# A gated state-space convolution and squared-ReLU MLP with all gradients: where one activation buffer lies, where the last row block of the MLP's backward pass is emitted, and a stored copy of (1-g)G

## The chip, the cores and the metric

The kernel runs on one core of a Trainium2 chip. Its metric is the device time of one execution in microseconds (us), as the median of several runs. Engines are called TensorE (PE in the profile), VectorE (DVE), ScalarE (ACT), GpSimd (POOL) and SyncE (SP).

## The reference

Inputs are u (2048 x 448, called x in the MLP), the parameters of a diagonal state-space model with 256 states for each of the 448 channels, the weights w1 (448 x 1792), b1, w2 (1792 x 448), b2, a gate vector and the gradient G of the output. Computed are the output and the gradients of all inputs:

```
g  = sigmoid(sum(x * gate_w))                     # one number per row
K  = Re(sum_n C * dB * exp(l * dt * A))           # a filter of 2048 taps per channel
a  = irfft(rfft(u, 4096) * rfft(K, 4096))[:2048] + u * Dskip
h  = relu(x @ w1 + b1);  b = (h * h) @ w2 + b2
out = g * a + (1 - g) * b
return out, vjp(out)(G)                           # out and its gradients
```

With L = 2048, D = 448, F = 1792, P = 128 there are LT = 16 row tiles, FT = 14 tiles of F, DT = 4 tiles of D; a row block is 512 rows, so there are four of them.

## The kernel before, in words

The program is written in a framework that gives each engine its own instruction order, worked out from the order in which the Python code emits the work and from data dependencies. Those become semaphore waits between engines. An `issue_after` forces one instruction to be placed after another. Memory comes as named tiles (X16, Y16, D16, U16, K28, R32, F17, P14, M8, S25), each of which exists once: taking the same tag again waits for the last users of the overlapping part of it. The profile names tiles by the first letter, so F is F17. PSUM is split into banks N0 to N3, X, S and the double bank F. SB is the tile S25, and RA is R32.

Stages, in order of time:

1. *FFT of u and of g·G (0 to about 190 us).* `fwd1` (L222) makes a first stage of matrix products, stores it to DRAM (gd), `load_s1` (L241) reads it back turned, `fwd2` (L243) makes the second stage; spectra are multiplied (`cmul`, L263 to L268) and transformed back (`inv1`, L270, to hd in DRAM). Between them transposes of u and of DB = (1-g)·G are stored (`transposed`, UT_d and DBT_d). DB itself is made at L518 by ScalarE in tile D16. `powers` (L588) makes records of powers of the state matrix in two sets of buffers, one of which lies in the tile F17 (`Fp`), and stores them as rec_d. The first row block of the MLP's hidden layer is made here: `hidden(0, jp, ...)` (L543, called at L647) does a matrix product into PSUM, then on ScalarE a Relu (L559) into a ring buffer r of 1024 columns and its square (L561) into SB; the ring buffer is stored to DRAM as rT_d by GpSimd (L565). The ring has two buffers: the end of the w1 tile in U16, and `Fp[:,7680:8704]`.
2. *K's gradient.* Constants Ew and Ew2 are loaded (L651 to L654, Ew2 in SB), hd is read back (`load_hs`, L291: tiles D and P), L671 sums it on TensorE into DK, which goes through DRAM (dk_d, L681 to L688).
3. *Recurrence (213 to 660).* A loop over 14 chunks of the states (L906). For each chunk VectorE builds tables X and Y from the records by products of powers (`build_x` and `build_y`, L715 to L776, with ScalarE's L756, L757, L765, L767 preparing factors in tile F); TensorE makes taps of K from them (`kgen`, L789; stored to k_d at L803) and the state gradients: `turn_yt` (L827, L828), `tables_t` (L815, L816), `back_z` (L857, L861), and `back_p` (L864), where VectorE forms products (L877, four per chunk) in buffers `Pr` and TensorE sums them (L886, 32 per chunk, sixteen for each half). Into this loop the scheduler mixes the MLP: forward (`hidden` and `project`, L936 to L948, results to br_d), w1 and w2 transposed (L969, L979), and backward (L996 to L1021). A backward row block is 56 matrix products dh = DB·w2^T (L1005, L1008) in banks N0 to N2, ScalarE's doubling (L1010), VectorE's product with r (L1017), which is read from rT_d into a ring `rr` (L993), GpSimd's store to dhT_d (L1018), and then `project` (56 matrix products, L946, evacuation L947, store to br_d L948).
4. *K's FFT.* The taps k_d are read back with 18 loads of SP (L1092 to L1097, tile X), a skip term is added (L1100), `fwd1` (L232) makes the first stage with a ring of 6 stage buffers in Y16 and P14, the stores go to gd, `load_s1` (L1182) reads them into K. At its end SP also loads spectra (R<-sp), the gradient (Y<-grad_out) and br_d. From L1107 on `act_only` is set, with which all evacuations of PSUM are ScalarE's.
5. *Products, inverse transforms, outputs, and the weights' gradients.* `grad_w2` (L1060) and `grad_w1` (L1065) call `gradrows` (L1051), sixteen matrix products (L1057) per tile of F; DB2 is DB once more, made from four loads of G into D16 and sixteen ScalarE scalings (L1084). `param_grads` (L1145) ends the program.

Of the kernel before, what the change touches and what calls it, by code (L numbers as in the profile page):

```python
# [19 lines left out]
P = 128  # L20
# [285 lines left out]
def kernel(ctx, tc, A_u, A_A_re, A_A_im, A_B_re, A_B_im, A_C_re, A_C_im, A_log_dt, A_Dskip,  # L306
# [17 lines left out]
    UT_d = dscr("UT_d", DP * L)  # L324
    k_d = dscr("k_d", VROW * D)
# [17 lines left out]
    def flat(ap):  # L343
        return ap.rearrange("p t d -> p (t d)")
# [172 lines left out]
    for t in range(LT):  # L517
        S.activation(DB[:, t, :], G[:, t, :], ACT.Copy, scale=omg32[:, t:t + 1])  # L518
    ps = K.ps("S", [P, 512])
# [127 lines left out]
    for jp in range(6):  # L647
        hidden(0, jp, NT[4:6], [w1v[:, 7168:8192], Fp[:, 7680:8704]])
# [64 lines left out]
    Pr = [b[:, 2048 * i:2048 * i + 2048].rearrange("p (s t g n) -> p s t g n", t=2, s=2, g=2) for b, k in ((Pt, 3), (P2, 1)) for i in range(k)]  # L713
# [150 lines left out]
    def back_p(c, XT, zb, gs, after):  # L864
# [8 lines left out]
        for r in range(2):  # L873
            pr = Pr[pi_ % 4]
# [58 lines left out]
    ring = [w1v[:, 7168:8192], Fv[:, 2048:3072], Fv[:, 3072:4096]]  # L933
    ni = 0

    def project(lb, w, hblk, ws, brs):  # L936
        nonlocal ni
        for tt in range(4):
            t = 4 * lb + tt
            br = brs[tt % len(brs)]  # L940
            ps = K.ps(NT[ni % 3], [P, 512])
# [3 lines left out]
            for j in range(FT):  # L945
                T_.matmul(ps[:, 0:D], lhsT=hblk[j][:, P * tt:P * tt + P], rhs=ws[:, j, :], start=(w == 1 and j == 0), stop=(j == FT - 1))  # L946
            S.copy(br, ps[:, 0:D])  # L947
            G_.dma_start(bass.AP(tensor=br_d, offset=(t * P * 2 + w) * D, ap=[[2 * D, P], [1, D]]), br)  # L948

# [33 lines left out]
    rr = [SB[:, 8320:9344], Fv[:, 2048:3072], Fv[:, 3072:4096], w2Tv[:, 7168:8192], hv[:, 7168:8192]]  # L983
# [12 lines left out]
    for lb in range(4):  # L996
        for jp in range(FT // 2):
            pss = []
            i = lb * (FT // 2) + jp
            for j in (2 * jp, 2 * jp + 1):  # L1000
                ps = K.ps(NT[ni % 3], [P, 512])
# [19 lines left out]
        project(lb, 1, [hblk[:, j] for j in range(FT)], w1T, [SB[:, 9344 + 448 * k:9792 + 448 * k] for k in range(3)])  # L1021


    U = K.t("U16", [P, LT, DP])
    G_.memset(U[:, :, D:D + 1], 1.0)
    Uv = U[:, :, 0:D]
    DB2 = K.t("D16", [P, LT, D])
    for g in range(NG):
        G_.dma_start(flat(DB2[32 * g:32 * g + 32]), tl(G2, g))
# [11 lines left out]
    def gradrows(w, j, nb):  # L1041
# [14 lines left out]
        for t in range(LT):  # L1056
            T_.matmul(ps[:, 0:width], lhsT=hh[:, t, :], rhs=(DB2[:, t, :] if w == 0 else U[:, t, 0:D + 1]), start=(t == 0), stop=(t == LT - 1))  # L1057
        return ps

    def grad_w2(j):  # L1060
        ps = gradrows(0, j, NB)
        S.copy(dw2s[:, j % 2], ps[:, 0:D])
        G_.dma_start(out_12[j * P:(j + 1) * P, :], dw2s[:, j % 2])

    def grad_w1(j, nb):  # L1065
        nonlocal ni
        ps = gradrows(1, j, nb)
# [15 lines left out]
    for t in range(LT):  # L1083
        S.activation(DB2[:, t, :], DB2[:, t, :], ACT.Copy, scale=omg32[:, t:t + 1])  # L1084
    nc.sync.dma_start(ct["F1BD"][:, 0:256], nc.inline_tensor(cs["F1K"].astype(ml_dtypes.bfloat16), name="c_F1K").ap())
    xs = K.t("X16", [P, LT, D])
    vp = rounded_positions().reshape(P, LT)
    for (p0, p1) in ((64, 128), (32, 64), (16, 32), (0, 16)):
        offs = vp[p0] - LT * p0
        assert all((vp[p] - LT * p == offs).all() for p in range(p0, p1))  # L1090
        j = 0
        while p0 > 0 and j < LT:  # L1092
            n_ = int((offs == offs[j]).sum())
            nc.sync.dma_start(xs[p0:p1, j:j + n_], bass.AP(tensor=k_d, offset=(LT * p0 + int(offs[j])) * D, ap=[[LT * D, p1 - p0], [0, n_], [1, D]]))
            j += n_
        if p0 == 0:
            nc.sync.dma_start(flat(xs[0:p1]), bass.AP(tensor=k_d, offset=0, ap=[[LT * D, p1], [1, LT * D]]))  # L1097
    xv = xs[:].rearrange("p l (j c e) -> p l c j e", j=2, e=32)

# [103 lines left out]
    for q in range(4):  # L1203
        if q < 3:
            K.fwd2(s1k[:, q + 1], q + 1, spk(q + 1))
# [153 lines left out]
```

## Time and profile before

| | us |
|---|---|
| median of three runs | 966.41 (956.93, 973.71, 966.41) |
| the profiled execution's own time | 964.21 |
| its span, from the first to the last instruction | 962.4 |
| busy: TensorE, VectorE, ScalarE, GpSimd | 720.2, 669.5, 608.0, 196.2 |
| DMA moved | 182.67 MB, a mean of 190 GB/s |

The mean granted TensorE clock was 0.823 of full speed. In the profile L12 is line 12 of the kernel's source. A line of a timeline has the start (us), the time that it took (us), the engine, the source line, the operation, the output tile, an arrow, the input tiles, the shape and the count. Brackets give how long the engine was idle before it, and what released it; "q" behind an engine's name (SPq, ACTq) is its issuing of DMAs. A row of the windows gives a stretch of time with the busy us of each engine, the granted clock, the busy share of the 16 DMA engines, and what they moved.

### The profile page before, as it was taken

The numbers are of one execution on the slowest core, as the hardware profiler recorded it, in microseconds if no ns is written. First come the engines' busy times: TensorE is split into PE (matmuls) and PEld (weight loads), VectorE is DVE, ScalarE is ACT, GpSimd is POOL, SyncE is SP. The second block draws the span as 40 slices with busy tenths as digits, with TensorE's granted clock in tenths as the row PEclk, the third lists the DMA queues.
The fourth block names the chain that finished last, engine by engine and source line by source line (L and its number), as shares of the span: only waits on it lengthen the run. The fifth ranks groups of instructions, "written<-read, shape, count | busy, mean of one in ns | idle before, by whom it ended". The sixth has DMA issues, their size and how long they took to land.

```text
span 962.4 us, 18900 instructions
## 1 busy us (share of the span) xinstructions
PE 720.2 (75%) x7593; PEld 337.6 (35%) x7593; DVE 669.5 (70%) x1139; ACT 608.0 (63%) x976; POOL 196.2 (20%) x328
## 2 busy tenths in 40 slices
PE   3747555656787879779779887999438789996885
PEld 1313111123433434435334434454212135542343
DVE  4775978619499999999689988873305873277900
ACT  0878557643868788786876575655256756565543
POOL 1424000210011212031023130325200012452310
PEclk9966655577678989989799797999758789998898
DMA  9998774793156644467339753828998996789531
GB/s 192 269 299 296 266 271 158 297 253 114 34 127 143 123 114 113 108 158 162 77 115 217 162 150 94 209 96 211 314 279 254 344 290 219 237 245 281 152 108 42
DMA packets 157615, 182.67 MB, mean 190 GB/s; under 512 B 89954, under 2 KB 133336, under 8 KB 156744
## 3 DMA queue, kind: packets, MB, share of 16 engines
q1 hardware_dynamic: 109492, 78.26, 33.7%
q0 software_dynamic: 21120, 65.42, 21.6%
q10 hardware_dynamic: 26916, 37.81, 11.7%
q8 instruction: 59, 0.97, 0.4%
q14 instruction: 28, 0.23, 0.1%
HBM read 90.12 MB, written 71.07 MB: 167 GB/s over the span
## 4 chain that ended last, share of the span: by engine, by line
issue 31%; PE 18%; DMA 16%; DVE 14%; ACT 11%; POOL 8%; ACTq 0%; SPq 0%; POOLq 0%; DVEq 0%
PE psF L1057 4%; DMA gd<-P 2%; DVE X L1158 2%; POOL rT_d L565 2%; PE psN L946 2%; POOL dhT_d L1018 1%; DMA gd<-R 1%; POOL br_d L948 1%; DMA prow<-in_B_b_dram 1%; DMA D<-s_d 1%; DMA K<-gd 1%; ACT S L1052 1%; DMA hd<-st 1%; PE psN L232 1%; PE psS L447 1%
## 5 line engine op out<-in xcount | busy, mean ns | idle before, releaser
L1057 PEld LDWEIGHTS <-S 128*128 128x128 bf16 x448 | 43.8, 103 | 62.4 <-issue 18.2
L861 ACT CAST R<-psF 128x1024 bf16<-128x1024 f32 x56 | 57.4, 1025 | 10.7 <-PE psF L857 10.7
L1005 PE MATMUL psN<-S,U 128*128 128x512 bf16 x168 | 52.2, 423 | 10.3 <-ACT D L1010 10.0
L1057 PE MATMUL psF<-D,S 128*128 128x448 bf16 x224 | 53.7, 387 | 6.3 <-ACT D L1084 3.6
L723 DVE TENSOR_TENSOR X<-X,F 128x512 bf16<-128x512 bf16 (+1 forms) x70 | 37.5, 536 | 28.5 <-ACT F L756 26.4
L554 PE MATMUL psN<-S,U 128*128 128x512 bf16 x132 | 44.2, 447 | 13.8 <-ACT F L559 13.4
L946 PE MATMUL psN<-D,S 128*128 128x448 bf16 x208 | 51.5, 384 | 0.0
L946 PE MATMUL psN<-S,D 128*128 128x448 bf16 x224 | 46.7, 359 | 1.7 <-ACT D L1010 1.7
L877 DVE TENSOR_TENSOR P<-R 128x2048 bf16<-128x2048 bf16 x35 | 41.5, 1218 | 5.1 <-ACT R L861 5.1
L857 PE MATMUL psF<-R,S 64*32 64x256 bf16 (+1 forms) x1344 | 35.7, 293 | 11.8 <-ACT R L861 4.1
L734 DVE TENSOR_TENSOR K<-K,F 128x2048 bf16<-128x2048 bf16 (+3 forms) x42 | 36.3, 865 | 10.7 <-ACT F L765 9.4
L1018 POOL DMA_DIRECT2D dhT_d<-D x28 | 20.3, 725 | 113.2 <-DVE D L1017 106.4
L1010 ACT ACTIVATE D<-psN 128x512 bf16<-128x512 f32 x56 | 31.1, 607 | 15.8 <-PE psN L1008 15.7
L251 PEld LDWEIGHTS <-M 128*64 128x64 bf16 x192 | 13.7, 130 | 69.5 <-issue 66.2
L735 DVE TENSOR_TENSOR F<-K,F 128x2048 bf16<-128x2048 bf16 (+3 forms) x42 | 35.9, 854 | 2.7 <-ACT F L767 2.7
L734 DVE TENSOR_TENSOR Y<-Y,F 128x2048 bf16<-128x2048 bf16 (+3 forms) x42 | 36.4, 866 | 1.7
L724 DVE TENSOR_TENSOR F<-X,F 128x512 bf16<-128x512 bf16 (+1 forms) x70 | 37.0, 528 | 0.6
L737 DVE TENSOR_TENSOR Y<-Y,F 128x2048 bf16<-128x2048 bf16 (+3 forms) x42 | 36.3, 865 | 1.3
L828 ACT COPY M<-psX 128x1024 bf16<-128x1024 bf16 x26 | 26.6, 1022 | 16.8 <-PE psX L827 16.8
L737 DVE TENSOR_TENSOR K<-K,F 128x2048 bf16<-128x2048 bf16 (+3 forms) x42 | 36.3, 864 | 1.3
L735 DVE TENSOR_TENSOR F<-Y,F 128x2048 bf16<-128x2048 bf16 (+3 forms) x42 | 35.9, 854 | 0.0
L263 DVE TENSOR_TENSOR F<-R,K 128x1792 bf16<-128x1792 bf16 x8 | 8.7, 1092 | 37.3 <-ACT K L206 35.4
(351 smaller groups left out, 1965.9 us busy)
## 6 DMA issues: line engine op xcount, KB each, us to landing
hd<-st ACTq DMA_DIRECT2D x20, 448.0 KB, 5.3
sp<-K ACTq DMA_DIRECT2D x8, 896.0 KB, 6.2
dhT_d<-D POOLq DMA_DIRECT2D x28, 256.0 KB, 4.9
R<-sp SPq DMA_DIRECT2D x8, 896.0 KB, 5.7
S<-rT_d POOLq DMA_DIRECT2D x14, 512.0 KB, 6.2
R<-hd SPq DMA_DIRECT2D x16, 448.0 KB, 7.7
S<-dhT_d POOLq DMA_DIRECT2D x14, 512.0 KB, 4.1
rec<-rec_d SPq DMA_DIRECT2D x14, 480.0 KB, 5.3
```

Source lines behind the costliest of these rows:

```text
L554: T_.matmul(ps[:], lhsT=w1w[:, dt, j * P:j * P + P], rhs=ub[:, dt], start=(dt == 0), stop=False, skip_group_check=True)
L723: V.tensor_tensor(out=hi4, in0=lo, in1=bcast_dims(pr, [0, (None, n), 1]), op=ALU.mult)
L724: V.tensor_tensor(out=Vv.rearrange("p (x a r) -> p x a r", x=2 * W2, r=2), in0=lo, in1=bcast_dims(pi, [0, (None, n), 1]), op=ALU.mult)
L734: V.tensor_tensor(out=hi, in0=lo, in1=bcast_dims(pr, [0, (None, n // 2), 1]), op=ALU.mult)
L735: V.tensor_tensor(out=Vv.rearrange("p (x a q) -> p x a q", x=rows, q=2), in0=lo, in1=bcast_dims(pi, [0, (None, n // 2), 1]), op=ALU.mult)
L737: return V.tensor_tensor(out=T4[:, :, :, n:2 * n], in0=T4[:, :, :, n:2 * n], in1=V4, op=ALU.add)
L857: T_.matmul(psz[32 * ii:32 * ii + m, t, 256 * s:256 * s + 256], lhsT=DKc[64 * t:64 * t + 64, s, g, 2 * ii:2 * ii + 1 + par].rearrange("p i ...
L861: S.copy(zb[:, :, :, gg].rearrange("p s t n -> p t s n"), psz[:].rearrange("p t (s n) -> p t s n", s=2))
L877: lastp = V.tensor_tensor(out=pr.rearrange("p s t g n -> p s t (g n)"), in0=zv, in1=(xb if r == 0 else rev_dim(xb, 2)), op=ALU.mult)
L946: T_.matmul(ps[:, 0:D], lhsT=hblk[j][:, P * tt:P * tt + P], rhs=ws[:, j, :], start=(w == 1 and j == 0), stop=(j == FT - 1))
L1005: T_.matmul(ps[:], lhsT=w2Tw[:, jp, dt, j % 2], rhs=dblk[:, dt], start=(dt == 0), stop=False, skip_group_check=True)
L1057: T_.matmul(ps[:, 0:width], lhsT=hh[:, t, :], rhs=(DB2[:, t, :] if w == 0 else U[:, t, 0:D + 1]), start=(t == 0), stop=(t == LT - 1))
```

## The change

It has four parts, called A to D here.

- A: in `hidden(0, jp)` for jp below 6 the second ring buffer is `SB[:, 11648:12672]`, no longer `Fp[:, 7680:8704]`. Ew2 lies in SB from column 10752 on.
- B: the ring `Pr` of `back_p` has three buffers, all in P14, instead of four. The first half of the tile P2 becomes two more buffers of the MLP's forward ring (three to five) and of the backward ring `rr` (five to seven).
- C: the backward loop becomes `row_block(lb, banks)`. Blocks 0 to 2 are emitted as before. Then come the loads of K's taps and K's `fwd1`, with eight stage buffers instead of six, and then row block 3 in the banks X, S and F. The first `fwd2` of K is placed after the last matrix product of that block. The evacuations of K's `fwd2` alternate between ScalarE and VectorE, as those of its `fwd1` do in both kernels; those of the products stay ScalarE's.
- D: DB is stored to DRAM (DB_d) by SP right after L518. DB2 is one GpSimd load from there, in U16; the four loads of G and the sixteen scalings go. U lies in D16 then, and `pgt` in U16.

```diff
+    DB_d = dscr("DB_d", L * D)
...
         S.activation(DB[:, t, :], G[:, t, :], ACT.Copy, scale=omg32[:, t:t + 1])
+    nc.sync.dma_start(bass.AP(tensor=DB_d, offset=0, ap=[[LT * D, P], [1, LT * D]]), flat(DB))
...
     for jp in range(6):
-        hidden(0, jp, NT[4:6], [w1v[:, 7168:8192], Fp[:, 7680:8704]])
+        hidden(0, jp, NT[4:6], [w1v[:, 7168:8192], SB[:, 11648:12672]])
...
-    Pr = [b[:, 2048 * i:2048 * i + 2048].rearrange("p (s t g n) -> p s t g n", t=2, s=2, g=2) for b, k in ((Pt, 3), (P2, 1)) for i in range(k)]
+    Pr = [b[:, 2048 * i:2048 * i + 2048].rearrange("p (s t g n) -> p s t g n", t=2, s=2, g=2) for b, k in ((Pt, 3),) for i in range(k)]
...
-            pr = Pr[pi_ % 4]
+            pr = Pr[pi_ % 3]
...
-    ring = [w1v[:, 7168:8192], Fv[:, 2048:3072], Fv[:, 3072:4096]]
+    ring = [w1v[:, 7168:8192], Fv[:, 2048:3072], Fv[:, 3072:4096], P2[:, 0:1024], P2[:, 1024:2048]]
...
-    def project(lb, w, hblk, ws, brs):
+    def project(lb, w, hblk, ws, brs, banks=NT[0:3]):
...
-            ps = K.ps(NT[ni % 3], [P, 512])
+            ps = K.ps(banks[ni % 3], [P, 512])
...
+        return lastm
...
-    rr = [SB[:, 8320:9344], Fv[:, 2048:3072], Fv[:, 3072:4096], w2Tv[:, 7168:8192], hv[:, 7168:8192]]
+    rr = [P2[:, 0:1024], P2[:, 1024:2048], Fv[:, 2048:3072], Fv[:, 3072:4096], SB[:, 8320:9344], w2Tv[:, 7168:8192], hv[:, 7168:8192]]
...
-    for lb in range(4):
+
+    def row_block(lb, banks):
+        nonlocal ni
...
-        project(lb, 1, [hblk[:, j] for j in range(FT)], w1T, [SB[:, 9344 + 448 * k:9792 + 448 * k] for k in range(3)])
+        return project(lb, 1, [hblk[:, j] for j in range(FT)], w1T, [SB[:, 9344 + 448 * k:9792 + 448 * k] for k in range(3)], banks)
+    for lb in range(3):
+        row_block(lb, NT[0:3])
+
+    nc.sync.dma_start(ct["F1BD"][:, 0:256], nc.inline_tensor(cs["F1K"].astype(ml_dtypes.bfloat16), name="c_F1K").ap())
+    xs = K.t("X16", [P, LT, D])
...
+    K.fwd1(lambda j: xv[:, j], gd[2], stage= [b_[:, 1792 * i:1792 * i + 1792].rearrange("p (a d) -> p a d", d=D) for b_, n_ in ((Yv, 4), (Pk_, 4)) for i in range(n_)])
+    lastw = row_block(3, ["X", "S", "F"])
+    DB2 = K.t("U16", [P, LT, D])
+    G_.dma_start(flat(DB2), bass.AP(tensor=DB_d, offset=0, ap=[[LT * D, P], [1, LT * D]]))
+    U = K.t("D16", [P, LT, DP])
...
-    DB2 = K.t("D16", [P, LT, D])
-    for g in range(NG):
-        G_.dma_start(flat(DB2[32 * g:32 * g + 32]), tl(G2, g))
...
-    for t in range(LT):
-        S.activation(DB2[:, t, :], DB2[:, t, :], ACT.Copy, scale=omg32[:, t:t + 1])
...
-    K.act_only = True
...
-    K.fwd2(s1k[:, 0], 0, spk(0))
+    K.act_only = False
+    with tc.issue_after(lastw.ins):
+        K.fwd2(s1k[:, 0], 0, spk(0))
     for q in range(4):
+        K.act_only = False
         if q < 3:
             K.fwd2(s1k[:, q + 1], q + 1, spk(q + 1))
+        K.act_only = True
         product(0, q, sx[q])
...
-    pgt = K.t("D16", [P, 8192])
+    pgt = K.t("U16", [P, 8192])
```

## The prediction, made before the changed kernel had run

> **What bounds the kernel now.** I read the page first, then the chain of work that ended last, the timelines of single engines around each place that the diff touches, and tables of busy time by window. No single engine bounds the program (VectorE 70% of the span, TensorE 75%), so each stage is read by itself. Three matter here.
>
> The first is the start of the recurrence. VectorE has nothing to do from 187.2 to 213.5:
>
> ```profile
> 213.54 0.43 DVE L723 TENSOR_TENSOR X<-X,F 128x512 bf16<-128x512 bf16 x1 [26.39 <-ACT F L756]
> ```
>
> ScalarE names why L756 came so late, twice:
>
> ```profile
> 201.80 0.69 ACT L559 ACTIVATE F<-psX,b_f 128x512 bf16<-128x512 f32 x1 [5.05 <-DMA rT_d<-F]
> ...
> 203.36 0.71 POOL L565 DMA_DIRECT2D rT_d<-F  x1 [6.69 <-ACT F L559]
> ...
> 211.84 0.63 ACT L756 ACTIVATE F<-rec 128x512 bf16<-128x512 bf16 x1 [7.69 <-DMA rT_d<-F]
> ```
>
> The first column is the start, the second the duration, the bracket the idle time before it and what ended it. Both L559's ring buffer and L756's table lie in tile F, which the store rT_d<-F reads; issued at 203.36 it lands 8.40 us later, and this DMA is a piece of the chain. But a second chain ends nearby: the K-gradient sums (L671) end at 229.06+0.35, their ten stores are issued by SP from 229.68, and the reload K<-dk_d holds ScalarE until 239.53, so that VectorE idles again:
>
> ```profile
> 239.53 1.01 ACT L828 COPY R<-psS 128x1024 bf16<-128x1024 bf16 x1 [5.33 <-DMA K<-dk_d]
> ```
> ```profile
> 255.38 0.41 DVE L734 TENSOR_TENSOR K<-K,F 128x256 bf16<-128x256 bf16 x1 [9.43 <-ACT F L765]
> ```
>
> From 258 to 470 VectorE bounds: in 300 to 320 it is busy 19.28 of 20 us, and so in every such window.
>
> The second stage is K's FFT, 660 to 724, where DMA is the resource (share is the mean of the 16 DMA engines):
>
> ```profile
> core 0: us, PE busy (x) PEld busy (x) DVE busy (x) ACT busy (x) POOL busy (x), PEclk, DMA share, GB/s
> 300.00:320.00 20.00, 18.88 (x319) 8.88 (x318) 19.28 (x33) 14.94 (x22) 6.95 (x12) 0.88 0.78 189
> ...
> 660.00:680.00 20.00, 15.61 (x78) 7.10 (x78) 3.28 (x6) 5.79 (x12) 10.13 (x19) 1.00 0.95 297
> 680.00:700.00 20.00, 10.15 (x44) 4.23 (x44) 8.04 (x14) 6.98 (x15) 3.78 (x7) 0.67 1.04 316
> 700.00:720.00 20.00, 6.71 (x28) 3.18 (x27) 0.00 (x0) 12.26 (x21) 1.88 (x3) 0.59 0.97 257
> ```
>
> TensorE does block 3's projection, then K's first FFT stage with holes, then waits:
>
> ```profile
> 664.27 10.77 PE L946 MATMUL psN<-S,D 128*128 128x448 bf16 x56
> 674.88 0.73 PE L232 MATMUL psN<-X,cb_F1BD 128*128 128x448 bf16 x3
> 680.49 2.46 PE L232 MATMUL psN<-X,cb_F1BD 128*128 128x448 bf16 x6 [4.88 <-ACT S L947]
> ...
> 694.93 2.06 PE L232 MATMUL psN<-X,cb_F1BD 128*128 128x448 bf16 x5 [6.19 <-DVE P L207]
> ...
> 723.62 1.70 PE L251 MATMUL psN<-K,M 128*64 128x448 bf16 x8 [13.00 <-DMA K<-gd]
> ```
>
> 4.88 us is a psum bank held while ScalarE waits for a br_d store (S buffers of L947), 6.19 us is a stage buffer held by a gd<-P store of 14.63 us, 13.00 us is the reload that may start only when the last gd store has landed (712.9). After it comes the third stage: VectorE's products (729.8 to 781), then TensorE, 19.62 of 20 us busy in 800 to 820.
>
> **The change, part by part** (minus is faster, us).
>
> *DB_d store, +2.5.* It adds 1.84 MB on SP, just ahead of Y<-gd (issued at 74.91). What it delays is the w1 load: issued 83.16, landing 5.84 later, with ScalarE idle 3.23 and VectorE 5.36 before it, so it is on the path. The DMA share was 0.55 in 70 to 75, 0.90 in 75 to 80, 0.99 to 1.01 from 80 to 90. The Trainium skill ("DMA: Bandwidth & Descriptors", section Issuing engines are not separate DMA queues) says that DMAs of SP, ScalarE and GpSimd run on the same 16 DMA engines and interleave. By that rule a store on an otherwise quiet SP queue isn't free: at the 337 GB/s of 80 to 85 it is 5.5 us of DMA time, and if nothing is idle all of it is paid. By the rows, 45% of 5 us and 10% of 5 us are idle before the w1 load (2.75 us), and the Ew2 load of 0.26 MB (0.8 us) goes out of the stretch: 5.5 - 2.75 - 0.8 = 2. I take 2.5, between 1 and 5.
>
> *r ring's second buffer out of F, -3.* L756/L757 of chunk 0 no longer wait for rT_d<-F. In the built order they stand between the L559 and L561 of hidden steps 2 to 5. L559 of the last step still waits for the store from two steps earlier, as now (201.80), so the fourth of these table operations ends near 203.1 + 0.6 = 203.7: VectorE can start about 213.5 - 203 = 10 sooner. Its own end of chunk 0 comes sooner by that, but chunk 1 needs K<-dk_d, thus L671. The new buffer S[11648:] overlaps Ew2 (L653), so that load waits for these r stores; in SP's built order it now stands ahead of the four P<-hd loads, which are queued behind it. Stores land about 211.8; then Ew2 (0.32 us of queue), P<-hd (2.70 us of queue as at 193.80). D<-hd took a median of 4.6 us to land and P<-hd 13.4 while queued among others: P lands 215 + 5 to 9 = 220 to 224 instead of 207.9. Then 42 L671 (4.2 us), the L946 of the same stretch (3.0) and the last 54 (3.2): end 230 to 234, against 229.4. So the K-gradient side slips by 1 to 5. What recovers some is ScalarE's order: L815's tables no longer hold L671 up (8.46 us of wait at 221.17, "DVE X L727"), three L828 come ahead of the dk_d reloads and an L816 goes behind L765 of chunk 1, four operations of 1.0 us, for one L757 of 0.6 that comes ahead: 3.4 less, and the 2.61 us that the fourth L828 waited for TensorE falls into the reload. Against a slip of 3 that is L765 at 251 instead of 254.1: -3, between -10 (all of VectorE's lead) and +4 (slip without recovery).
>
> *Three power buffers instead of four, +2.5.* VectorE's fourth L877 of a chunk now reuses the first's buffer and so waits for the 16 L886 of the chunk's first half. In the trace of before the fourth L877 begins at 304.6 and those L886 end at 308.4 (3.8 late), 332.4 against 334.6 (2.2), 415.8 against 420.2 (4.4), 443.7 against 446.7 (3.0), below 1 elsewhere but for chunk 8, where VectorE idles 12.35 us next anyway. Behind the waiting L877 the whole VectorE queue stands, here the next chunk's L743 and L723, and ScalarE and TensorE then wait for those. If TensorE keeps its pace, the delay is the largest of these, 4.4, not their sum of 15, and the 12.35 us hole at 473 can swallow it: +2.5, between 0 and 15.
>
> *Deeper rings (3 to 5, 5 to 7 buffers), 0.* No L559 between 258 and 460 waits for a DMA, and L1017 waits for ScalarE's L1010 (23.2 us in seven waits), not for a load. At most -2.
>
> *Block 3 behind K's first FFT, -8.* In the built order TensorE finishes the recurrence, runs block 3's 56 L1005/L1008, then alternates its 56 L946 with the 32 L232. Taken out of the recurrence's tail (TensorE 18.86 of 20 us busy in 640 to 660), those 56 let the last L886 and the k_d stores come some 3 to 8 earlier than 659.5; they then run beside the X<-k_d loads, some 16 us at 0.28. L946 and L232 together are 10.8 + 32 x 0.35 = 22 us, so the first stage ends near 655 + 16 + 22 = 693, instead of 701; the 4.88 us hole is filled by the other's matmuls, and eight stage buffers (for six) take away part of the 6.19 and 2.27. The gd stores must still drain: the DMA share is already 0.95 to 1.04. What leaves the stretch ahead of K<-gd is Y<-grad_out and one R<-sp, put behind it in SP's order, and the U<-in_A_u load: 1.84 + 0.90 MB at 300 GB/s is 9, less what is only reordered within POOL's queue. K<-gd thus starts at 705 (712.9), lands 10.7 later: -8, between -13 (TensorE's own gain plus the drained bytes) and 0 (DMA as saturated as now). L1084's sixteen ScalarE scalings vanish (3.63 us of wait for grad_w2); the store costed above pays for them. The load U<-DB_d has the bytes of those it replaces: 0.
>
> *Filling the wait, -3.* About one more grad_w2 (16 x 0.387 = 6.2 us) fits before K's second stage, and is then missing from 785 to 840, where TensorE bounds. Half is kept. The skill ("TensorE: Matmul & The Clock Gate", Part 1) has the clock fall to half after an idle window of about 3.4 us. The row: 0.59 granted in 700 to 720, 0.72 in 720 to 740, against 0.96 in 740 to 760. If the hole closed, the 13.81 us of 720 to 740 would become 10.4 (an estimate: 13.81 x 0.72/0.96). A wait for K<-gd of over 3.4 us stays in my timeline, so by the rule this brings nothing; I take 0.
>
> *Evacuation of K's second stage split, 0.* Half of the 32 copies (0.44 on ScalarE) go to VectorE (0.58 by L207's row): the first product may start 2 earlier, but VectorE gains 16 x 0.58 = 9.3 us within its product chain, which has 5.3 idle in 740 to 760 and 0.7 in 760 to 780. Between -3 and +5.
>
> Sum: 2.5 - 3 + 2.5 - 8 - 3 = -9. The profiled execution took 964.21 (span 962.4, 1.8 around it), 2.2 below the median of the three runs shown. 964.2 - 9 + 2.2 = 957.
>
> **Rivals.**
> *The whole recurrence lead is kept.* If P<-hd lands as fast as D<-hd, L671 ends at 229 and VectorE's 10 us come through to chunk 1; with the same K stage and the hole closed (-3.4): 957 - 7 - 3.4 = 946.6, and 943 if the ring costs nothing either. For it: only one DMA stands on the chain there. Against it: 9.43 us of idle shows another release.
> *DMA bounds K's stage and nothing is won there.* Share 0.95 to 1.04 for it. The K terms are then 0, the start gives 2: 968. Against it: TensorE's own holes before the stores are issued.
> *The three buffers stall VectorE in every chunk (slower).* Place: the fourth L877, 212 us of a VectorE-bound stage. If TensorE's order puts the first half's L886 as late as in chunk 2 or 6 each time, and the delay is handed on (VectorE late, so the tables late, so TensorE late), 13 x 4 = 52, less the 2.5 counted: 957 + 49.5 = 1006. It decides once the mean stall is over (9 + 2.5)/13 = 0.9 us a chunk, and by 2% from 2.4. Against it: in half of the chunks the trace has it below 1.
> *The change doesn't do what it says:* rT_d<-S may hold the same L756 through another tile. In the built order L756 waits for no such store, so I give this nothing of its own.
>
> **How the numbers follow.** Forecast (957, its own range 946 to 967) 0.46; lead kept (943 to 947) 0.24; DMA-bound (968) 0.18; stalls in every chunk (975 to 1006) 0.12. Under 2% can hardly be told from no change, the three runs alone span 957 to 974. Faster by over 2% means below 947.1: four fifths of the second case and a fifth of the first, 0.28. Slower means above 985.7: most of the last case, 0.1. The rest, 0.62, is within. The range leaves out the far part of the second case and two thirds of the last: 936 to 980.
>
> **What would show it.** Right: L723 of chunk 0 starts near 203 to 206 and no L756 waits for a DMA; L671 ends 230 to 236; in 300 to 460 VectorE still has 19 of 20 us, with L877 waits on "PE" of under 5 in all; K<-gd starts by 706 on the new time scale less the early gain; L232 and L946 alternate. Wrong: L877 waits of 2 or more in most chunks; P<-hd landing after 226; K<-gd no earlier than now relative to the last L886, with the DMA share still at 1; VectorE's products longer than 55 us; or VectorE idle over 9 before the w1 load lands.

## The result, and the profile after

| | before | after |
|---|---|---|
| median (runs) | 965.17 us (15) | 950.6 us (12) |
| ratio, 95% interval | | 0.9904 (0.9869 to 0.9939) |
| profiled execution: span | 962.4 us | 947.8 us |
| VectorE, ScalarE busy | 669.5, 608.0 us | 679.3, 594.0 us |
| DMA moved | 182.67 MB | 184.51 MB |

Some executions of every kernel are longer than the rest, most of them at a lower granted clock; the medians count all, the ratios leave out those over 1.5% above the kernel's fastest, and the traces of two runs below (no_B and again) are of such executions and are not read.

A second set of runs of the changed kernel gave the same ratio, 0.9904 (0.9862 to 0.9946), with a median of 954.09 beside 963.41. The change is worth 1% (0.0096 x 965 = 9.3 us), and the forecast of 957, 9 us below its base, is right in sign and size; how much of that was luck is told at the end.

In the changed source the lines lie two further down in the recurrence (L723 is L725, L756 is L758, L877 is L879, L886 is L888) and more behind it (L946 is L948, L1005 is L1010, L1010 is L1015, L1017 is L1022, L1057 is L1085).

**Where the time went, by marks that are in both traces.** The first 70 us are alike in both kernels but not in both executions: (1-g)G (L518) is complete at 71.3 in the trace of before and at 66.6 in that of after. Over all traces of this study it varies from 65.5 to 71.3. So I count from that mark. The next marks are the recurrence's last state product (L886), the first product of K's second stage (L251), the end of the 224th gradient product (the last of dw2), and the end.

| us | (1-g)G to last L886 | to K's second stage | to 224th product | to the end | sum |
|---|---|---|---|---|---|
| before | 588.5 | 63.8 | 113.1 | 125.7 | 891.1 |
| after | 593.0 | 55.2 | 108.6 | 124.3 | 881.2 |
| difference | +4.5 | -8.6 | -4.5 | -1.3 | -9.9 |

The recurrence loses 4.5, and K's stage and what follows win 14.4. The sum of -9.9 agrees with the ratio; the spans alone (-14.6) contain 4.7 us of a luckier beginning.

How far can one trace be trusted? Up to the last L886 the kernels of four runs below (params_early, six_stage, no_fill, no_split) have the same instructions in the same order as after. Their traces give 593.6, 595.5, 595.9 and 596.4 for a stretch that is 593.0 in after. So a stretch of this length varies by some 3.4 us, after's is the shortest of five, and the recurrence loses 4.5 to 7.9. Behind the start of K's second stage five runs (no_A, r_apart, r_apart_4, six_stage, best) share after's order: 106.3 to 110.8 to the 224th product, and 123.7 to 127.9 from there to the end.

*The start of the recurrence.* VectorE's timeline after (start, duration, and in brackets the idle time before it with what ended it):

```profile
199.50 0.43 DVE L725 TENSOR_TENSOR X<-X,F 128x512 bf16<-128x512 bf16 x1 [9.11 <-ACT F L758]
207.11 0.43 DVE L726 TENSOR_TENSOR F<-X,F 128x512 bf16<-128x512 bf16 x1 [7.18 <-ACT F L759]
...
249.34 0.42 DVE L726 TENSOR_TENSOR F<-X,F 128x512 bf16<-128x512 bf16 x1 [12.23 <-ACT F L759]
```

No wait for rT_d<-F is left here: 213.5 became 199.5 (9.3 earlier counted from the mark), with a second hole to 207.1, since the four table operations are spread over ScalarE's r steps. The last of them stands behind a square that still waits for a store of r, now from the new place:

```profile
205.29 0.69 ACT L561 ACTIVATE S<-psX,b_f 128x512 bf16<-128x512 f32 x1 [4.88 <-DMA rT_d<-S]
```

The third wait is chunk 1's, where L734 stood waiting for L765 until 255.4. What it waits for begins on SP and TensorE:

```profile
209.51 0.33 SPq L655 DMA_DIRECT2D S<-c_Ew  x1
209.89 2.62 SPq L291 DMA_DIRECT2D P<-hd  x4
```
```profile
223.50 0.56 PE L673 MATMUL psN<-P,M 128*32 128x448 bf16 x1 [6.11 <-DMA P<-hd]
```

Ew2 (S<-c_Ew) is issued only when the r stores that read its place have landed, and P<-hd behind it: TensorE gets its data at 223.5 instead of 207.9. The K-gradient sums end at 234.6 (229.4), and ScalarE's L765 of chunk 1 begins at 251.2 (254.1): counted from the mark that is 9.9 and 1.9 later.

*The three power buffers.* In after's recurrence VectorE waits three times for TensorE's sums, where before it had no such wait. The other traces with three buffers have two to seven such waits, in each one of 7.2 to 9.3 us near 480; those with four buffers have none:

```profile
304.72 1.23 DVE L879 TENSOR_TENSOR P<-R,P 128x2048 bf16<-128x2048 bf16 x1 [1.59 <-PE psN L888]
362.77 1.23 DVE L879 TENSOR_TENSOR P<-R,P 128x2048 bf16<-128x2048 bf16 x1 [2.39 <-PE psN L888]
481.56 1.23 DVE L879 TENSOR_TENSOR P<-R,P 128x2048 bf16<-128x2048 bf16 x1 [7.58 <-PE psN L888]
```

The 7.58 stands in the hole of 12.35 that VectorE had at 473 in any case. The waits ahead of it are 4.0 us here, and 3.8 to 6.0 in the five traces of this order. In chunks 1, 2, 3, 6 and 7 these sums end at most 0.4 us before the fourth L879 begins, so VectorE now runs at TensorE's pace there. Counted from the mark, VectorE is 1.9 us behind the kernel before at chunk 1, 7.1 at chunk 6 (its fourth L877 at 446.1 and 443.7), and 4.9 at the next chunk but one (514.1 and 513.9): the waits cost 4.0, and the hole takes back 2.2.

*K's stage.* The windows of after (columns as before):

```profile
660.00:680.00 20.00, 20.00 (x94) 8.15 (x94) 11.91 (x20) 11.58 (x23) 9.83 (x16) 1.00 0.79 242
680.00:700.00 20.00, 14.18 (x86) 7.40 (x84) 1.33 (x3) 7.63 (x14) 4.41 (x9) 0.91 1.04 350
700.00:720.00 20.00, 6.97 (x31) 2.43 (x29) 2.55 (x5) 3.75 (x6) 1.49 (x3) 0.67 1.03 355
```

TensorE is busy for all 20 us from 660 to 680 (15.61 before) at the full clock. Its timeline shows the projection and K's first stage in turns, then one and a half gradient rows, then the reload:

```profile
670.02 0.36 PE L948 MATMUL psF<-S,D 128*128 128x448 bf16 x1
670.22 0.54 PE L232 MATMUL psN<-X,cb_F1BD 128*128 128x448 bf16 x2
...
694.70 4.17 PE L1085 MATMUL psF<-U,S 128*128 128x448 bf16 x16 [0.26 <-ACT S L1080]
...
700.76 1.69 PE L1085 MATMUL psF<-U,S 128*128 128x448 bf16 x8 [0.67 <-ACT S L1080]
714.80 1.71 PE L251 MATMUL psN<-K,M 128*64 128x448 bf16 x8 [12.36 <-DMA K<-gd]
```

The first stage ends at 688.2 (701.0), K<-gd is issued at 704.8 (712.9), and 24 gradient products are done before K's second stage instead of 10. The last wait is as long as before (12.36 and 13.00): the hole has moved up and has not closed.

### The profile page after: what moved, and what is told of

Its sections match the earlier page's. It is cut to its first block, busy times and chain, and to the rows that moved or that the text cites. A ratio compares the mean times of both kernels' runs of the same rounds, so it can differ in the third digit from the quotient of the medians.

```text
span 947.8 us, 18859 instructions
## 1 busy us (share of the span) xinstructions
PE 711.7 (75%) x7593; PEld 337.8 (36%) x7593; DVE 679.3 (72%) x1155; ACT 594.0 (63%) x944; POOL 195.4 (21%) x325
## 2 busy tenths in 40 slices
DMA packets 157711, 184.51 MB, mean 195 GB/s; under 512 B 89922, under 2 KB 133304, under 8 KB 156712
## 4 chain that ended last, share of the span: by engine, by line
PE 28%; DVE 22%; DMA 20%; ACT 17%; issue 8%; SPq 2%; POOL 2%; ACTq 0%; POOLq 0%; DVEq 0%
PE psN L948 4%; PE psF L1085 3%; DVE F L737 2%; PE psX L791 2%; ACT R L863 2%; PE psX L829 2%; DVE X L1162 2%; DMA rec<-rec_d 2%; PE psN L251 2%; PE psF L859 2%; SPq L397 2%; DVE P L879 1%; DMA P<-hd 1%; PE psN L556 1%; DMA gd<-P 1%
## 5 line engine op out<-in xcount | busy, mean ns | idle before, releaser
L1085 PEld LDWEIGHTS <-S 128*128 128x128 bf16 x448 | 43.3, 103 | 66.4 <-issue 22.0
L863 ACT CAST R<-psF 128x1024 bf16<-128x1024 f32 x56 | 57.2, 1021 | 12.7 <-PE psF L859 12.7
L1085 PE MATMUL psF<-U,S 128*128 128x448 bf16 x224 | 54.7, 391 | 6.8 <-ACT S L1080 6.6
L879 DVE TENSOR_TENSOR P<-R 128x2048 bf16<-128x2048 bf16 x42 | 49.4, 1218 | 6.6 <-ACT R L863 6.6
L207 DVE CAST K<-psN 128x448 bf16<-128x448 f32 x36 | 21.8, 620 | 43.7 <-PE psN L251 42.6
L556 PE MATMUL psN<-S,U 128*128 128x512 bf16 x132 | 41.8, 428 | 14.0 <-ACT M L561 9.0
L859 PE MATMUL psF<-R,S 64*32 64x256 bf16 (+1 forms) x1344 | 40.1, 316 | 14.9 <-DMA R<-K 4.9
L948 PE MATMUL psN<-D,S 128*128 128x448 bf16 x208 | 48.8, 372 | 0.5 <-ACT S L566 0.5
L1010 PE MATMUL psN<-S,U 128*128 128x512 bf16 x126 | 38.7, 421 | 10.9 <-ACT D L1015 9.6
L725 DVE TENSOR_TENSOR X<-X,F 128x512 bf16<-128x512 bf16 (+1 forms) x70 | 37.4, 534 | 11.4 <-ACT F L758 9.1
L206 ACT CAST K<-psN 128x448 bf16<-128x448 f32 x36 | 18.3, 526 | 31.1 <-PE psN L251 31.1
L251 PEld LDWEIGHTS <-M 128*64 128x64 bf16 x192 | 14.5, 139 | 65.3 <-issue 62.6
L948 PE MATMUL psN<-S,D 128*128 128x448 bf16 x168 | 36.2, 362 | 1.8 <-ACT D L1015 1.6
L859 PEld LDWEIGHTS <-S 64*16 64x16 bf16 (+1 forms) x1792 | 22.9, 92 | 39.0 <-issue 21.0
```

Of the source, the lines that this page charges most:

```text
L556: T_.matmul(ps[:], lhsT=w1w[:, dt, j * P:j * P + P], rhs=ub[:, dt], start=(dt == 0), stop=False, skip_group_check=True)
L725: V.tensor_tensor(out=hi4, in0=lo, in1=bcast_dims(pr, [0, (None, n), 1]), op=ALU.mult)
L859: T_.matmul(psz[32 * ii:32 * ii + m, t, 256 * s:256 * s + 256], lhsT=DKc[64 * t:64 * t + 64, s, g, 2 * ii:2 * ii + 1 + par].rearrange("p i ...
L863: S.copy(zb[:, :, :, gg].rearrange("p s t n -> p t s n"), psz[:].rearrange("p t (s n) -> p t s n", s=2))
L879: lastp = V.tensor_tensor(out=pr.rearrange("p s t g n -> p s t (g n)"), in0=zv, in1=(xb if r == 0 else rev_dim(xb, 2)), op=ALU.mult)
L948: lastm = T_.matmul(ps[:, 0:D], lhsT=hblk[j][:, P * tt:P * tt + P], rhs=ws[:, j, :], start=(w == 1 and j == 0), stop=(j == FT - 1))
```

## The experiments

The theory after the first reading of these traces: the recurrence gives back what part A wins, to the power buffers and the store of (1-g)G; the gain is made in K's stage, by the order (C), and by what TensorE can do there while it waits (D). The first four runs each undo one part. In the table the ratio is to the kernel before on the same chip, and the stages are those above. The runs come from three chips, so kernels are compared by the ratios, not by the medians.

| run | median us (runs) | ratio (95% interval) | to last L886 | to K's 2nd stage | to 224th | to the end |
|---|---|---|---|---|---|---|
| after | 950.6 (12) | 0.9904 (0.9869, 0.9939) | 593.0 | 55.2 | 108.6 | 124.3 |
| again | 954.1 (12) | 0.9904 (0.9862, 0.9946) | | | | |
| no_A | 959.2 (12) | 0.9940 (0.9907, 0.9974) | 597.5 | 54.2 | 106.9 | 124.7 |
| no_B | 955.2 (6) | 0.9867 (0.9804, 0.9929) | | | | |
| no_C | 956.0 (12) | 0.9897 (0.9862, 0.9932) | 597.5 | 67.2 | 98.5 | 123.8 |
| no_D | 962.5 (12) | 0.9939 (0.9896, 0.9981) | 588.3 | 51.6 | 121.3 | 132.5 |
| r_apart | 946.3 (6) | 0.9849 (0.9776, 0.9921) | 591.2 | 53.9 | 107.6 | 123.7 |
| r_apart_4 | 943.1 (6) | 0.9814 (0.9759, 0.9869) | 583.9 | 54.6 | 106.3 | 123.7 |
| params_early | 962.0 (12) | 0.9995 (0.9957, 1.0032) | 593.6 | 55.5 | 121.2 | 126.0 |
| no_fill | 968.2 (12) | 1.0039 (1.0008, 1.0071) | 595.9 | 56.7 | 117.4 | 132.8 |
| no_split | 970.7 (12) | 1.0015 (0.9972, 1.0058) | 596.4 | 55.1 | 112.3 | 134.8 |
| six_stage | 950.8 (6) | 0.9811 (0.9760, 0.9862) | 595.5 | 50.0 | 110.8 | 127.9 |
| best | 942.3 (6) | 0.9755 (0.9715, 0.9794) | 576.9 | 54.3 | 109.7 | 124.8 |

**again** is the changed kernel itself.

> The changed kernel once more, unaltered, as the base for the runs beside it on the same chip: 946 to 955 us by every theory. If what was read from one trace is steady: the recurrence ends near 660, the 224th gradient product (the last of dw2) near 823, and the end lies 124 us behind that product.

Its times agree with the first set, and so does its ratio. Whether the marks hold still can't be read from its trace.

**no_A**

```diff
-        hidden(0, jp, NT[4:6], [w1v[:, 7168:8192], SB[:, 11648:12672]])
+        hidden(0, jp, NT[4:6], [w1v[:, 7168:8192], Fp[:, 7680:8704]])
```

> The changed kernel with part A undone alone: the second ring buffer of r is in the powers' tile again, the rest stays. Theory (what the changed recurrence wins at its start is given back in a hole of VectorE near 473, so that A is worth next to nothing by the end; the gain is part C's): 949 to 953 us, VectorE's first L723-type product back near 211 to 214, the last K-gradient product near 229 instead of 234.6, the last L886-type product of the recurrence within 1.5 us of the changed kernel's 659.6. Rival (A carries part of the 14.6 us): 955 to 960, the recurrence ends 4 us or more later.

VectorE starts at 215.4 after a wait of 26.54 again. Counted from the mark the sums end 4.9 earlier than after's, and still L765 of chunk 1 comes 2.9 later; VectorE is 2.9 later at chunk 6, and the recurrence is 4.5 longer (597.5). That is only 1.1 longer than the longest of the five traces of after's order. The ratio is 0.0036 above that of after, some 3.5 us, with intervals that overlap. The median lies where the rival had it, and A is worth some 1 to 4.5 us; that it is worth more than nothing is likely and not shown.

**no_B**: `Pr` from P14 (three) and P2 (one), `pi_ % 4`, and both rings as before.

> The changed kernel with part B undone alone: four power buffers, rings of three and five. Theory (the three buffers cost VectorE 4.0 us in two waits, which the hole near 473 swallows): no wait of L877's line for TensorE's sums is left between 262 and 480, VectorE is 2 to 5 us earlier at chunk 6, and the recurrence still ends within 1.5 us of 659.6; 948 to 952 us. Rival 1 (the stalls are handed on to the end): 944 to 947. Rival 2 (the deeper rings are worth something): 954 to 958.

Six runs from 947.7 to 972.9 don't tell the sides apart. The ratio is 0.0037 below after's, some 3.6 us, with intervals that overlap; the pair r_apart and r_apart_4 below has the traces to it.

**no_C**

```diff
-    for lb in range(3):
-        row_block(lb, NT[0:3])
+    for lb in range(4):
+        lastw = row_block(lb, NT[0:3])
...
-    lastw = row_block(3, ["X", "S", "F"])
```

> The changed kernel with block 3 emitted ahead of K's first stage again, in banks N0 to N2 (A, B, D, the eight stage buffers and the split evacuation stay). Theory (the order is the gain): K's second stage starts at 721 to 725 as before the change instead of 714.8, and the time is 959 to 965 us. Rival (the gain is due to more stage buffers, to traffic that is gone or to the split): it starts before 718 and the time is 950 to 955.

TensorE's timeline of no_C has the old hole back (ScalarE's L949 waits 8.28 us for br_d<-S, as before the change), and K's second stage comes 67.2 us behind the recurrence:

```profile
687.96 2.46 PE L232 MATMUL psN<-X,cb_F1BD 128*128 128x448 bf16 x6 [6.21 <-ACT S L949]
...
712.42 3.17 PE L1084 MATMUL psF<-U,S 128*128 128x448 bf16 x8 [11.86 <-ACT S L1079]
```

That is 12 us more than after, and the recurrence, which contains block 3 again, is 4.5 longer. Yet the ratio is that of after: the start missed both forecasts, and the median is just above the rival's. The trace shows what gives most of it back: 48 gradient products instead of 24 stand before the second stage (all of them from 712.42 on), and the next stretch is 10.1 shorter. So the start of K's second stage, on which the prediction placed its largest term, isn't by itself the end's clock. How many products TensorE has behind it at that time counts as much. By the ratios C alone, with D and the split in place, is worth nothing that can be measured here; by this one trace it is some 6.

**no_D**

```diff
-    nc.sync.dma_start(bass.AP(tensor=DB_d, ...), flat(DB))
...
-    G_.dma_start(flat(DB2), bass.AP(tensor=DB_d, ...))
+    for g in range(NG):
+        G_.dma_start(flat(DB2[32 * g:32 * g + 32]), tl(G2, g))
+    for t in range(LT):
+        S.activation(DB2[:, t, :], DB2[:, t, :], ACT.Copy, scale=omg32[:, t:t + 1])
```

> The changed kernel with the copy of (1-g)G undone alone: no store after the first transposes; four loads of G into the same tile U16 and sixteen ScalarE scalings at the same place. Theory (the store costs 1 to 4 us of the first stage; the scalings lie in the time in which TensorE waits for K's reload): 947 to 950 us, first VectorE product of the recurrence 1 to 4 us earlier. Rival 1 (the store lies in idle DMA time and costs nothing): 950 to 952. Rival 2 (the scalings are on the path at K's stage): 953 to 957.

The recurrence is 4.7 shorter without the store (4.7 to 8.1 against the five traces) and K's second stage 3.6 nearer, and still the run isn't shorter: the ratio is 3.4 us above that of after, with intervals that overlap. In TensorE's order no gradient product stands before K's second stage now, and it waits:

```profile
708.38 2.31 PE L251 MATMUL psN<-K,M 128*64 128x448 bf16 x10 [18.61 <-DMA K<-gd]
```

The scalings take 9.05 us of ScalarE at 691, DB2 is ready at 700, but the products have been placed behind that wait. The stretch to the 224th product is 12.7 longer and the last one 8.2. Rival 2 had the direction, but the median of 962.5 is beyond its 957, and the scalings themselves end before the reload has landed. With them, and the loads of G ahead of them, the scheduler placed the filling work later.

**r_apart** and **r_apart_4**

```diff
-        hidden(0, jp, NT[4:6], [w1v[:, 7168:8192], SB[:, 11648:12672]])
+        hidden(0, jp, NT[4:6], [w1v[:, 7168:8192], SB[:, 11776:12800]])
```

> The changed kernel with the second r buffer moved on by 128 columns, so that it no longer overlaps the constants Ew2, and the P<-hd loads no longer queue behind that load. Theory (the queue behind the r stores is what makes the K-gradient sums end at 234.6): Ew2 is loaded near 88 again, P<-hd lands near 208, the sums end at 222 to 229, L765 of chunk 1 is 3 to 7 us earlier. If the recurrence hands that on, it ends 3 to 6 us earlier and the time is 944 to 948; if the hole near 473 swallows it, it ends within 1.5 us and the time is 949 to 952. Rival (L671 waits for VectorE's first tables in any case): nothing moves.

> As r_apart, and with four power buffers and the old rings (part B undone). Theory (three buffers cost 4 us of stalls, and the end of the recurrence follows VectorE): 3 to 5 us earlier than r_apart at the recurrence's end, 940 to 946 us. Rival (the stalls are swallowed by the hole): the same as r_apart within 1.5 us at the recurrence's end.

r_apart: Ew2 is issued at 89.8 again and P<-hd at 197.7, no product of the sums waits for P<-hd. Counted from the mark, the sums end 5.7 earlier than after's, and L765 of chunk 1 comes 5.6 earlier. So by these traces the queue behind the r stores takes more than A brings (2.9 there). But the lead is 5.5 at chunk 6, 4.2 after chunk 8 (where VectorE waits 8.45 us for TensorE's sums), and 1.8 at the end of the recurrence. With four buffers (r_apart_4) TensorE's sums are waited for nowhere, and the lead over after is 6.2 at chunk 1, 10.2 at chunk 6, 9.7 after chunk 8 and 9.1 at the end: 7.3 more than with three. The hole at 473 is there as well, in r_apart_4's VectorE timeline:

```profile
476.08 0.69 DVE L1022 TENSOR_TENSOR D<-D,S 128x1024 bf16<-128x1024 bf16 x1 [10.61 <-ACT D L1015]
```

Before, that row stood at 485.24 (12.35). Counted from the mark it comes 4.8 earlier, and VectorE's lead over the kernel before at chunk 6 is 3.0. The hole moves along with a lead, and so doesn't swallow it. By the ratios the step from three to four buffers is 3.4 us, with intervals that overlap, and no_B against after gives 3.6; by these two traces it is 7.3, but r_apart_4's is of its shortest execution (937.2).

**params_early**: the twelve loads of the state parameters for `param_grads` go into K's tile, so that they need not wait for the 224th product.

```diff
-    praw = pgt[:, 0:6144].rearrange("p (k t n) -> p t k n", k=6, t=DT)
+    praw = s1k[:, 0:2].rearrange("p q a d -> p (q a d)")[:, 0:6144].rearrange("p (k t n) -> p t k n", k=6, t=DT)
...
```

> The changed kernel with the state parameters for the last gradients (twelve loads) put into the first half of K's tile, free after the products, instead of into DB2's tile, and the two sums' buffers of M8 and U16 swapped between the odd and the even parts. Theory (the end of the kernel hangs on these loads, which wait for the last product of dw2: 124 us from there to the end in five of six traces): VectorE's parameter part begins and ends 10 us or more earlier and the time is 936 to 944. Rival (TensorE's work that is left sets the end): the loads come early, the end moves by less than 3 us, 947 to 952.

VectorE's products with the parameters (L1162) begin at 812.0 instead of 836.1, and its parameter part ends at 900.0 instead of 902.5. But the run is 1% longer, so both sides missed the time. TensorE's waits, from 715 on, by who was waited for (total, times, longest), show where it went:

```profile
PE psN L282 <- ACT st L206: 11.1, 3, 10.5
```

After has 1.8 in that row. In 780 to 800 TensorE is busy 9.48 us (16.26 after) with a DMA share of 1.04. The loads now run in a stretch where the DMA engines are full. That they hold up TensorE there fits the rows but wasn't separated, and every engine's order from K's second stage on is another one than after's. That the end hangs on these loads alone is refuted.

**no_fill**: the first gradient product of dw2 is placed behind the first of K's four second-stage parts.

```diff
+    f2 = K.lastmm
...
+            with tc.issue_after(f2.ins) if w == 0 and j == 0 else nullcontext():
+                lastm = T_.matmul(ps[:, 0:width], lhsT=hh[:, t, :], rhs=(DB2[:, t, :] if w == 0 else U[:, t, 0:D + 1]), ...)
```

> The changed kernel with one order added: the first gradient product of dw2 is placed behind the last product of the first of K's four second-stage parts, so that none of the 24 products that ran before K's second stage can run there. Theory (what counts for the end is how many of these products TensorE has done before K's second stage; from the runs so far each is worth about 0.42 us): K's second stage starts as before (54 to 56 us behind the recurrence's last product) and the end is 8 to 11 us later, 960 to 964. Rival (TensorE has room for them later, in the product stage; the start of K's second stage sets the end): less than 3 us later, 950 to 955.

K's second stage starts 56.7 behind the recurrence, near after's 55.2; the time is 968.2, and the ratio 1.0039: all of the change's gain is gone, and more than the theory had said (13 us by the two ratios, instead of 8 to 11). The stretch to the 224th product is 8.8 longer (24 products, 0.37 each), and the last stretch 8.5 longer, which the count of products doesn't explain. (The trace is of an execution of 975.7, so these two are rather too long.)

**no_split**: `act_only` is True for K's `fwd2` too.

> The changed kernel with the evacuations of K's second stage on ScalarE alone again. Prediction's term: 0 (between the split being worth 3 us and costing 5): 949 to 955. Rival (the split is part of the gain): 956 to 960. Rival (VectorE's sixteen copies of 0.6 us lengthen its product chain): 944 to 948.

The median is 970.7, far above every expectation; by the ratios undoing the split costs 1.1% of the time, 10.7 us. To K's second stage nothing changes (55.1). Behind it VectorE's products (L263 to L268), first and last, are in after and then in no_split:

```profile
719.87 1.08 DVE L263 TENSOR_TENSOR F<-R,K 128x1792 bf16<-128x1792 bf16 x1
787.47 1.09 DVE L268 TENSOR_TENSOR P<-F 128x1792 bf16<-128x1792 bf16 x1
```
```profile
723.30 1.09 DVE L263 TENSOR_TENSOR F<-R,K 128x1792 bf16<-128x1792 bf16 x1 [39.68 <-ACT K L206]
785.84 1.09 DVE L268 TENSOR_TENSOR P<-F 128x1792 bf16<-128x1792 bf16 x1
```

Counted from the start of K's second stage (714.8 and 717.0) they end at 73.8 with the split and 69.9 without. So the second rival was right in the chain: VectorE has sixteen copies more, 9.9 us in all, and the chain is 3.8 us longer. What no_split loses lies elsewhere: the stretch to the 224th product is 3.7 longer, the last one 10.5. Read instruction by instruction, no_split's last stretch has the same order on all five engines as no_fill's (132.8), and another one than after's, which no_A, r_apart, r_apart_4, six_stage and best share (123.7 to 127.9). So the edit didn't undo the split alone: the scheduler built everything behind it in another order, and so it did for no_fill. The two orders differ, among much else, in a row of VectorE's waits from the 224th product on that is 4.2 in after; no_split's:

```profile
DVE X L1162 <- DMA U<-in_A_C_re_dram: 9.5, 1, 9.5
```

It is 9.3 in no_fill, 5.6 in no_D, 6.0 before. Which of the moved instructions costs the time is open, and so is what the split is worth in one order.

**six_stage**: `(Yv, 4), (Pk_, 2)` for the stage ring.

> The changed kernel with six stage buffers for K's first stage instead of eight. Theory (the waits for a stage buffer, 6.19 and 2.27 us before the change, go because of the two buffers more): TensorE waits 3 us or more for an evacuation into a stage buffer, the first stage ends 3 to 6 us later, K's second stage starts 1 to 4 later, 952 to 956. Rival (DMA sets the start of the second stage): it starts within 1 us, 950 to 953.

TensorE waits 2.92 us for a stage buffer and its first stage ends 2.7 later, near what the theory had. But K<-gd is issued 44.9 us behind the recurrence's last product, and 45.2 in after. The two buffers more bring nothing to that moment. (That DMA sets it, as the rival had it, fits.) The reload then landed in 5.1 us instead of 10.0, so the second stage started 5.2 earlier, which neither side forecast. The ratio, 0.9811, is even below after's, with intervals that don't overlap; from six executions on another chip I read no more than "not slower". This trace has the hole closed: TensorE waits 0.45 us for K<-gd instead of 12.36. These are the 20 us from the start of the second stage in after and in six_stage, with the granted clock behind the busy times:

```profile
714.80:734.80 20.00, 18.87 (x114) 7.49 (x113) 15.79 (x19) 11.50 (x21) 3.53 (x6) 0.86 1.02 278
```
```profile
712.26:732.26 20.00, 16.38 (x114) 7.16 (x113) 16.26 (x19) 11.40 (x21) 3.53 (x6) 1.00 1.04 309
```

The same 114 products take 16.38 us instead of 18.87. The prediction had put 3.4 on that, for the case that the hole closes.

**best**: r_apart_4 with the store elsewhere.

```diff
-    nc.sync.dma_start(bass.AP(tensor=DB_d, ...), flat(DB))
...
     spectra(0)
+    G_.dma_start(bass.AP(tensor=DB_d, ...), flat(DB))
+    Pct = K.t("D16", [P, 2, 4, 2, D])
```

> r_apart_4 (r's second buffer clear of Ew2, four power buffers, the old rings) with the store of (1-g)G moved from SP's queue ahead of the first reloads to GpSimd's queue behind the first reload of the other spectrum, where the DMA share was 0.35. Theory (the store cost the start 2.8 us by holding up the w1 load and the reloads): VectorE's first product of the recurrence 2 to 4 us earlier, the recurrence ends 2 to 4 us before that of r_apart_4, 936 to 943. Rival (the bytes cost the same wherever they are moved): as r_apart_4, 941 to 946.

The trace has the recurrence 7.0 shorter than r_apart_4's, more than the store had been thought to cost; by the ratios 5.7 us lie between the two. The ratio is 0.9755 (0.9715 to 0.9794), better than the kernels before and after, while its interval overlaps that of r_apart_4: what the other place of the store adds isn't settled.

## Why the prediction was right, point by point

- *DB_d store, +2.5 (1 to 5).* The mechanism holds and the size was low. The idle time of VectorE ahead of the w1 load, on which the term rested, before and after:

```profile
90.69 0.43 DVE L615 SCALAR_TENSOR_TENSOR R<-R 128x256 f32<-128x256 f32 x1 [5.36 <-ACT F L611]
```
```profile
92.51 0.43 DVE L617 SCALAR_TENSOR_TENSOR R<-R 128x256 f32<-128x256 f32 x1 [11.73 <-ACT F L613]
```

  It is 9.34 with the store and r in F (no_A) and 7.80 without the store and r in SB (no_D). So the store adds 4.0, in either place of r, and the new place 2.4. The second was missed: the new r buffer lies in the part of SB from which the transposes are stored, and ScalarE's first use of it waits for a store that shares the DMA engines with DB_d. From after's ScalarE timeline, then no_D's:

```profile
88.53 0.69 ACT L561 ACTIVATE S<-psX,b_f 128x512 bf16<-128x512 f32 x1 [7.08 <-DMA DBT_d<-S]
```
```profile
86.51 0.69 ACT L560 ACTIVATE S<-psX,b_f 128x512 bf16<-128x512 f32 x1 [3.16 <-DMA DBT_d<-S]
```

  At the recurrence's end the store costs 4.7 to 8.1 (no_D). The rule cited in the prediction, that all queues share the 16 engines, charged 5.5 for it, the idle shares of the rows left 2. The measured cost lies nearer to the rule: of the 3.5 us that were counted as free, at most 1.5 were.
- *r ring out of F, -3 (-10 to +4).* The term was worked out without the store, so no_D shows it. Counted from the mark P<-hd comes 14.6 later than before the change (12 to 16 forecast), the sums end 3.1 later (1 to 5), and L765 of chunk 1 begins 2.9 earlier (3). With the store (after) these are 20.3 and 9.9 later, outside the bounds, and L765 1.9 later. At the recurrence's end A is worth 1.1 to 4.5 (no_A). L765 itself varies by 4.2 over the five traces of after's order, so the close agreement of -2.9 is partly luck.
- *Three buffers, +2.5 (0 to 15).* 3.4 and 3.6 by two pairs of ratios, each with overlapping intervals, 7.3 by one pair of traces: inside the bounds, and rather low. That the delay is the largest wait and not their sum, and that the hole takes one of them, is roughly what after's trace shows (4.0 in two waits ahead of the hole, 2.2 of it taken back). The error: a ring that is short by one didn't cost a fixed stall here. It tied VectorE to TensorE's pace, so it ate the lead that r_apart had won (5.5 at chunk 6, 1.8 at the end). The lead is what A brings, and the two terms can't be added.
- *Rings, 0.* Not separated from the buffers.
- *Block 3 behind K's first stage, -8 (-13 to 0).* K's second stage starts 8.6 nearer to the recurrence's last product. The hole of 4.88 went, as said. "Take away part of the 6.19" by eight buffers: with six, 2.92 of it is left, and the reload is issued no later. That the recurrence's tail is shorter without block 3 (3 to 8) fits no_C (1.1 to 4.5). The terms within are right, but no_C also shows that most of a later start is made good by gradient products that are done meanwhile.
- *Filling the wait, -3.* Mis-sized: "half is kept". From before to after 14 products more stand ahead of the second stage and the stretch behind it is 4.5 shorter, 0.32 each, four fifths of a product's 0.39 (the prediction had half). In no_fill, 24 products cost 8.8 in that stretch, 0.37 each; the rest of its 13 lies in the last stretch, with the other order there. The wait that stays, over the 3.4 us of the rule that the prediction cites, is there (12.36), with 0.67 granted in 700 to 720 and 0.86 in the 20 us behind it. With the hole closed (six_stage) 1.00 is granted in those 20 us, so setting the clock's term to 0 fits both.
- *Split evacuation, 0 (-3 to +5).* In the chain that the prediction looked at, its account holds: VectorE's copies make the products end 3.8 later (no_split). But undoing the split costs 10.7 in all, mostly in the last stretch, where the prediction looked for nothing. That stretch has another order of instructions then, so the 10.7 is the price of both together.
- *L1084 and the DB2 load, 0.* "The store costed above pays for them": without the copy the run is not shorter, although the recurrence is, because the products that fill the wait lose their place.

Three of the prediction's signs of being wrong came: VectorE idle over 9 ahead of the w1 load (11.73), P<-hd behind 226 (223.5, or 228.2 on the scale of before), and products of over 55 us (68.7, from 51.5). The last contains a new wait of 7.76 us for R<-sp. The stretch to the 224th product is shorter all the same.

The start (forecast +2, with the three buffers) came out at +4.5 to +7.9, for the most part by the store, and K's stage and the rest (forecast -11) at -14.4: errors of opposite sign. That the total was met so closely is luck. The terms that were undone one by one don't add up either: in no_split and in no_fill the whole gain is gone, and both have the other order at the end. The case "whole lead is kept" was refuted for the changed kernel; r_apart_4, with another place for r and a fourth buffer, ends its recurrence 4.6 ahead of the kernel before, not 10. The case of stalls in every chunk didn't occur: after has three waits in thirteen chunks.

## What to carry to other kernels

When a buffer is moved to free one tile, ask of the new place who else reads or fills it, and which queue that waiter stands in: here it held one constant's load, and with it four loads behind it. A buffer ring that is one short can cap a lead won ahead of it, so cost the two together and not as a sum. While TensorE waits for a reload, the work that stands before that wait in its order shortens the stretch behind it by most of its length (0.32 and 0.37 of 0.39 us a product here); count it in the built order for each variant. And when one line is undone, look whether the rest of the order is still the same before its price is put down to that line.

## What the runs showed that was not expected

- The 224th gradient product is followed by the end after 123.7 to 127.9 us in after and the five runs with its order, and after 132.8 and 134.8 in no_fill and no_split, which share another. (Before, no_C, params_early and no_D have orders of their own: 125.7, 123.8, 126.0 and 132.5.) The lengths go with the orders; that the order alone makes them was not run, and what in it costs the 9 us is open.
- Two edits that look unrelated, the place of one gradient product and the engine of sixteen copies, led the scheduler to the same order 100 us later, and either took the whole gain of the change (13 and 10.7 us of 950).
